# A planned attention and feed-forward kernel: a DMA ring model in its planner, shared tail casts, more XN buffers, and AV one unit late

## The chip, the cores and the metric

The kernel runs on one core of a Trainium2 chip. The metric is the device time of one execution in microseconds (us). An execution counts as slow when it is over 1.5% above the fastest of the same kernel (or when a die runs at a lower clock); only fast ones are compared.

The engines are TensorE (PE; its weight loads are shown apart as PEld), VectorE (DVE), ScalarE (ACT), GpSimd (POOL) and SyncE (SP). SP issues every DMA of this kernel, in one fixed order.

## The reference

Attention in a window of 32 positions to each side, for 8 batches of 576 tokens with 8 heads of 64, then a feed-forward layer of 512 to 2048 to 512 on all 4608 tokens.

```python
scores = (q @ k.transpose(0, 1, 3, 2)) / sqrt(64)        # q, k, v: (8, 8, 576, 64) float32
scores = where(abs(i - j) <= 32, scores, -1e9)
x = softmax(scores) @ v                                  # then (4608, 512)
r = maximum(x @ w_in, 0)                                 # w_in: (512, 2048)
out = (s * r * r + b) @ w_out                            # w_out: (2048, 512)
```

## The kernel before

No engine's program is written down by hand. Each operation is added to a graph with a cost, the data that it reads and writes, and a key (its priority). A planner in the kernel, ordinary Python that runs while the kernel is built, orders the graph: at each step it takes the task that can start first by its estimates. The result is one fixed list for each engine. On the chip every engine runs its list in order and waits on semaphores, so a wrong estimate can't give a wrong result, but a task that stands too early makes everything behind it wait.

```python
def plan(self, rounds=5):
    self.land = {}
    for _ in range(rounds):
        self._order()          # make the lists, with the landing times of the last round
        self._rings()          # serve the DMAs first in, first out: new landing times

# in _rings, for each DMA served:
    self.land[j[0].n] = now + 1100.0 - j[0].start      # kept relative to the DMA's start

# in _order, for each task taken:
    free[t.stream] = st + t.cost
    if t.dma is not None:
        t.fin = st + self.land.get(t.n, t.cost + 1800.0 + t.dma[1] * t.dma[2])
    ...
    elif t.dma is not None:
        r = t.fin + 100.0 + u.slack                    # when a user of the data may start
```

Here `t.dma[1]` is the number of units of a transfer and `t.dma[2]` the ns of one unit.

Batches 0 and 1 are transposed on PE. For batches 2 to 7, Q and K come in pieces of 512 and 64 rows: a load into STG, a cast to bf16 into NAT, a DMA transpose, and for K a reordering copy on POOL. V has its own loads and casts. A unit is a tile of 128 positions: its scores go through the exponential (ACT) and the mask (DVE), then AV multiplies them with V, DVE normalizes into one of the XN buffers, and a transpose (on PE for batches 0 to 2, by DMA after that) puts the result into XT for the feed-forward layer.

```python
NSTG, NNAT, NEX, NXN, NR1, NOUT, XR = 8, 6, 5, 3, 3, 6, 2048
LAG = 2                                   # AV of unit u rides with the scores of unit u+2
for name in names:                        # chunk(): "q" and "k", for 512 rows and for 64 rows
    add("sp", ... load STG ..., 500.0, dma=("l", np_ // 2, 53.0))
    add("dve", ... cast STG to NAT, 2048 wide ..., 110 + 0.53 * 2048, slack=3000.0)
    add("sp", ... transpose NAT ..., dma=("t", np_, 22.0))
    ... POOL copies of K, slack=2000.0
```

The softmax here doesn't subtract the row's maximum and nothing guards it: scores larger than these inputs give would overflow.

## Time and profile before

| | before |
|---|---|
| median of 3 runs, later of 4 | 333.91 us, 333.4 us |
| span of the profiled execution | 332.1 us |
| PE busy, idle | 305.5 us, 26.6 us |

The view by stretches of the kernel before, in four stretches; the columns are the stretch and its length in us, busy us (and instructions) of PE, PEld, DVE, ACT and POOL, the granted PE clock, the DMA share and GB/s.

```profile
0.00:60.00 60.00, 46.77 (x992) 37.30 (x992) 40.05 (x84) 31.78 (x53) 27.20 (x42) 1.00 1.02 303
60.00:105.00 45.00, 42.88 (x515) 24.29 (x516) 34.06 (x62) 19.55 (x30) 10.39 (x10) 1.00 1.07 207
105.00:165.00 60.00, 52.71 (x628) 24.61 (x627) 42.19 (x86) 29.61 (x44) 10.45 (x10) 0.94 0.92 194
165.00:180.00 15.00, 15.00 (x153) 7.14 (x151) 11.06 (x21) 6.59 (x10) 0.00 (x0) 1.00 1.29 216
```

The length less the PE column is PE's idle time: 13.23, 2.12, 7.29 and 0 us. After 180 us PE is idle for 4.0 us more, nearly all of it the tail.

### The profile page before, as it was taken

How to read it: one execution, taken by the hardware profiler on the slowest of the kernel's cores; microseconds unless marked ns; L12 is line 12 of the kernel's file. 1: busy time of each engine (PE TensorE's matmuls, PEld its weight loads, DVE VectorE, ACT ScalarE, POOL GpSimd, SP SyncE). 2: the span in 40 equal slices, each digit the busy share in tenths (PEclk: the TensorE clock that was granted, in tenths of full speed). 3: DMA queues.
4: the chain of work that ended last, by engine and by line, in shares of the span. 5: the costliest groups of instructions: out<-in, count | busy, mean ns of one | idle time of the engine just before them, and what ended most of it. 6: DMA issues, size and time to landing. Idle time of an engine off the chain costs nothing.

```text
span 332.1 us, 8135 instructions
## 1 busy us (share of the span) xinstructions
PE 305.5 (92%) x3452; PEld 162.2 (49%) x3452; DVE 204.7 (62%) x396; ACT 141.1 (42%) x219; POOL 59.0 (18%) x72
## 2 busy tenths in 40 slices
PE   3687999899989996988999999999999999999995
PEld 3565787654445443433445444444544444444442
DVE  2865768857887884858667865995654443333321
ACT  4644574246435653543444444444544323333300
POOL 3446444005050004100500600040000000000000
PEclk9999999999999999899799999999999999999999
DMA  7999999899999966998899879973121111100021
GB/s 255 288 307 353 335 273 343 145 200 238 197 179 310 222 139 116 287 149 172 245 211 172 208 210 201 169 192 113 45 59 49 49 43 44 53 33 34 34 84 74
DMA packets 104581, 56.71 MB, mean 171 GB/s; under 512 B 77216, under 2 KB 96160, under 8 KB 104544
## 3 DMA queue, kind: packets, MB, share of 16 engines
q1 hardware_dynamic: 104544, 56.18, 72.8%
q8 instruction: 27, 0.44, 0.6%
q14 instruction: 10, 0.08, 0.1%
HBM read 36.70 MB, written 9.44 MB: 139 GB/s over the span
## 4 chain that ended last, share of the span: by engine, by line
PE 58%; DMA 28%; DVE 6%; issue 3%; SPq 2%; POOL 1%; ACT 1%; DVEq 0%
PE o L815 28%; PE w L797 24%; DMA stg<-in_k_dram 7%; DMA vst<-in_v_dram 6%; DMA stg<-in_moe_w_out_dram 5%; DMA xt<-xn 3%; PE avn L597 3%; DMA stg<-in_moe_w_in_dram 2%; DMA qt<-nat 2%; DVE gt L806 2%; DVE nat L504 2%; DMA ktr<-nat 1%; PE o L838 1%; PE sc L541 1%; DVE xn L619 1%
## 5 line engine op out<-in xcount | busy, mean ns | idle before, releaser
L815 PE MATMUL o<-wout,gt 128*128 128x512 bf16 (+1 forms) x640 | 146.2, 361 | 2.8 <-DVE gt L806 1.8
L797 PE MATMUL w<-xt,win 128*128 128x512 bf16 (+3 forms) x704 | 147.9, 346 | 0.9 <-ACT xt L631 0.9
L804 ACT ACTIVATE r<-w 128x512 bf16<-128x512 f32 (+2 forms) x152 | 87.2, 574 | 111.0 <-PE w L797 90.9
L806 DVE TENSOR_TENSOR gt<-r 128x512 bf16<-128x512 bf16 (+2 forms) x152 | 68.9, 459 | 69.8 <-ACT r L804 69.3
L815 PEld LDWEIGHTS o<-wout,gt 128*128 128x128 bf16 x640 | 61.6, 98 | 65.9 <-DVE gt L806 2.3
L797 PEld LDWEIGHTS w<-xt,win 128*128 128x128 bf16 x704 | 60.8, 100 | 58.5 <-issue 2.4
L518 POOL COPY kt<-ktr 128x512 bf16<-128x512 bf16 (+1 forms) x30 | 31.8, 1059 | 135.2 <-DMA ktr<-nat 134.1
L567 ACT ACTIVATE ex<-sc 128x1024 bf16<-128x1024 f32 (+1 forms) x35 | 35.7, 1021 | 35.3 <-PE avn L597 33.9
L828 DVE SCALAR_TENSOR_TENSOR outs<-o,sb,cvec 128x512 f32<-128x512 f32 (+1 forms) x40 | 27.4, 690 | 13.0 <-PE o L815 13.0
L504 DVE CAST nat<-stg 128x2048 bf16<-128x2048 f32 (+1 forms) x24 | 29.7, 1246 | 7.2 <-DMA stg<-in_k_dram 6.0
L597 PE MATMUL avn<-vb,ex 64*64 64x65 bf16 x976 | 22.1, 199 | 8.4 <-DVE xn L619 4.5
L571 DVE TENSOR_TENSOR ex<-ex,mask 128x1024 bf16<-128x1024 bf16 (+1 forms) x35 | 25.8, 739 | 2.4 <-ACT ex L567 1.1
L619 DVE TENSOR_TENSOR xn<-avn,rec 128x512 bf16<-128x512 f32 (+1 forms) x34 | 23.3, 686 | 4.7 <-DMA xt<-xn 3.9
L597 PEld LDWEIGHTS avn<-vb,ex 64*64 64x64 bf16 x976 | 14.4, 108 | 23.5 <-issue 8.7
L445 DVE CAST vb<-vst 128x512 bf16<-128x512 f32 (+1 forms) x32 | 14.5, 456 | 8.3 <-DMA vst<-in_v_dram 8.3
L541 PE MATMUL sc<-qt,kt 64*64 64x128 bf16 x504 | 14.9, 217 | 0.0
L617 DVE RECIPROCAL rec<-avn 128x8 f32<-128x8 f32 (+1 forms) x34 | 6.8, 200 | 8.1 <-PE avn L597 8.1
L465 PE MATMUL w<-ident,nat 64*64 64x64 bf16 x144 | 5.4, 239 | 6.2 <-ACT nat L458 4.5
L541 PEld LDWEIGHTS sc<-qt,kt 64*64 64x64 bf16 x504 | 9.8, 107 | 1.3 <-issue 0.9
L426 POOL CAST win<-stg 128x1024 bf16<-128x1024 f32 x8 | 8.5, 1068 | 8.9 <-DMA stg<-in_moe_w_in_dram 8.8
L631 ACT COPY xt<-avn 128x512 bf16<-128x512 bf16 (+1 forms) x9 | 4.8, 537 | 11.6 <-PE avn L626 11.6
L465 PEld LDWEIGHTS w<-ident,nat 64*64 64x64 bf16 x144 | 4.6, 151 | 6.9 <-ACT nat L458 4.5
(62 smaller groups left out, 96.8 us busy)
## 6 DMA issues: line engine op xcount, KB each, us to landing
vst<-in_v_dram SPq DMA_DIRECT2D x32, 256.0 KB, 5.4
out_dram<-outs SPq DMA_DIRECT2D x32, 256.0 KB, 2.2
stg<-in_q_dram SPq DMA_DIRECT2D x6, 1024.0 KB, 6.6
stg<-in_k_dram SPq DMA_DIRECT2D x6, 1024.0 KB, 11.2
stg<-in_moe_w_in_dram SPq DMA_DIRECT2D x8, 512.0 KB, 7.6
stg<-in_moe_w_out_dram SPq DMA_DIRECT2D x8, 512.0 KB, 9.1
stg<-in_q_dram SPq DMA_DIRECT2D x8, 288.0 KB, 5.7
stg<-in_k_dram SPq DMA_DIRECT2D x8, 288.0 KB, 6.1
```

The lines of the kernel that those rows point to most:

```text
L504: add("dve", lambda e, stg=stg, nat=nat: e.tensor_copy(nat.rearrange("p (i h d) -> p h i d", h=H, i=4), stg.rearrange("p (h i d) -> p h i ...
L518: add("pool", lambda e, c=c, w=w: e.tensor_copy(KT[slot][:, :, c:c + w].rearrange("p a (s i) -> p a s i", i=4), KTR[slot][:, :, :, c // 4: ...
L541: fns = [lambda e, pr=pr, j=j, hp=hp: e.matmul(SC[64 * (j % 2):64 * (j % 2) + 64, hp, pr * 128:pr * 128 + 128], lhsT=KT[slot][64 * hp:64 * ...
L567: add("act", lambda e, dst=flat_dst, src=flat_src: e.activation(dst, src, AF.Exp, bias=0.0, scale=0.125), 190 + 0.833 * 512 * len(hs), rea ...
L571: add("dve", lambda e, flat=flat, mask=mask: e.tensor_tensor(flat, flat, mask, ALU.mult), 130 + 0.53 * 512 * len(hs), reads=[("E", ei, hp, ...
L597: return [lambda e: e.matmul(av[64 * x:64 * x + 64, h, 0:D + 1], lhsT=buf[64 * g:64 * g + 64, h % 2, h // 2, c:c + 64], rhs=VB[slot][64 * ...
L619: add("dve", lambda e: e.tensor_tensor(XN[xi][0:p1, :].rearrange("p (a c) -> p a c", a=H), av[0:p1, :, 0:D], REC[ri][0:p1, :].rearrange("p ...
L797: add("pe", [lambda e, g=g, kc=kc: e.matmul(wt[:, g, :], lhsT=WIN_BF[:, kc, (f0 + g) * 128:(f0 + g + 1) * 128], rhs=XT[:, kc, t0 % XR:t0 % ...
L804: add("act", lambda e: e.activation(rt, wt, AF.Relu, bias=0.0, scale=1.0), 190 + 0.833 * ng * nt, reads=[("W", wb)], writes=[("R1", rb)], ...
L806: add("dve", lambda e: e.tensor_tensor(GT[gs][:, f0:f0 + ng, g0:g0 + nt], rt, rt, ALU.mult), 130 + 0.53 * ng * nt, reads=[("R1", rb)], wri ...
L815: add("pe", [lambda e, fc=fc: e.matmul(O[:, ob, 0:cn], lhsT=GT[gs][:, fc, g0:g0 + 128], rhs=WOUT_BF[:, fc, c0:c0 + cn], start=(fc == 0), s ...
L828: add("dve", lambda e: e.scalar_tensor_tensor(OUTS[us][:, 0:cn], O[:, ob, 0:cn], SB128[:, 0:1], CVEC[:, c0:c0 + cn], ALU.mult, ALU.add), 2 ...
```

## The change

Its intent: fewer and shorter casts on DVE, lists that put DMA-dependent work later, and buffers where DVE had to wait. It has five parts.

1. The planner models a full DMA ring: a DMA blocks SP until all but 160 of the units asked for so far, its own included, have been served. SLACK lets users of transfers start later still; some of the planner's costs (transposes, K copies) and the casts' key change a little too.
2. The 64-row tails of Q and K are loaded into one buffer and share a cast. Every cast is cut into two halves of 1024; those of batch 2 go to POOL.
3. Five XN buffers for three, five output buffers for six.
4. AV one unit late and not two.
5. New pacing of the loads.

```diff
-LAG = 2
+LAG = 1
-PACE = ((-1,-1,-1,-1),(-2,-2,-2,-2),(-2,-2,-2,-2))
+PACE = ((-1, -1, -1),) * 3
+CASTS = 20.0
+CASTE = (("pool", "pool"), ("dve", "dve"))
+SLACK = (3000.0, 4000.0, 5000.0, 5000.0)
+    RING = 160.0
     def plan(self, rounds=5):
-        self.land = {}
+        self.land, self.block = {}, {}
 ...  in _rings: note what the queue has served at each time, then
+        for t, upto in asked:
+            while i < len(served) and served[i][1] < upto - self.RING:
+                i += 1
+            if i < len(served):
+                self.block[t.n] = max(0.0, served[i][0] - t.start)
 ...  in _order:
-            free[t.stream] = st + t.cost
+            free[t.stream] = st + max(t.cost, self.block.get(t.n, 0.0))
-        NSTG, NNAT, NEX, NXN, NR1, NOUT, XR = 8, 6, 5, 3, 3, 6, 2048
+        NSTG, NNAT, NEX, NXN, NR1, NOUT, XR = 8, 6, 5, 5, 3, 5, 2048
 ...  chunk() becomes piece(); the third piece holds both tails:
+            for i, parts in enumerate(((("q", 0, 512, 0),), (("k", 0, 512, 0),), (("q", 512, 64, 0), ("k", 512, 64, 32)))):
+                piece(b, parts, key + 0.01 * i, [paced(b, PACE[min(b, 4) - 2][i])])
```

More of the change, by code (lines that the diff above doesn't have):

```diff
@@ L107, in _rings @@
         jobs = {"hw": [], "sw": []}
+        self.block = {}
+        served, asked, total = [(0.0, 0.0)], [], 0.0
         for t in self.order:
@@ L110, in _rings @@
                 r = "sw" if t.stream == "pool" else "hw"
+                if r == "hw":
+                    total += t.dma[1]
+                    asked.append((t, total))
                 jobs[r].append([t, t.start + t.cost + (300.0 if r == "hw" else 700.0), float(t.dma[1])])
@@ L124, in _rings @@
             now += step
+            if "hw" in live:
+                served.append((now - step, served[-1][1]))
+                served.append((now, served[-1][1] + step / cost))
             for r, j in live.items():
@@ L129, in _rings @@
                     at[r] += 1
+        i = 0
+        for t, upto in asked:
[3 more added lines that the diff above has]
+                self.block[t.n] = max(0.0, served[i][0] - t.start)
     def _order(self):
@@ L481, in q_later, with piece @@
             return QTS[b % 2].rearrange("p (i a) s -> p i a s", i=4)
-        def chunk(b, t0, n, key, names="qk"):
-            slot, np_, s0 = b % 2, n // 4, t0 // 4
-            if b < 4 and t0 == 0 and "q" in names:
+        def piece(b, parts, key, waits):
+            slot = b % 2
+            ring["stg"] += ring["stg"] % 2
+            ring["nat"] += ring["nat"] % 2
+            si, _ = take("stg", NSTG), take("stg", NSTG)
+            ni, _ = take("nat", NNAT), take("nat", NNAT)
+            stg = STGS[:, si:si + 2, :].rearrange("p x c -> p (x c)")
+            nat = NATS[:, ni:ni + 2, :].rearrange("p x c -> p (x c)")
+            stgr, natr = [("STG", si), ("STG", si + 1)], [("NAT", ni), ("NAT", ni + 1)]
+            top = max(p0 + n // 4 for _, _, n, p0 in parts)
+            add("sp", [lambda e, name=name, t0=t0, n=n, p0=p0: e.dma_start(
+                stg[p0:p0 + n // 4, :].rearrange("p (h c) -> p h c", h=H),
+                src_of[name][b, :, t0:t0 + n, :].rearrange("h (p i) d -> p h (i d)", i=4))
+                for name, t0, n, p0 in parts],
+                500.0 * len(parts), writes=stgr, key=key - 20.0, waits=waits,
+                dma=("l", sum(n for _, _, n, _ in parts) // 8, 53.0))
+            for x in (0, 1):
+                eng = CASTE[min(b, 3) - 2][x]
+                add(eng, lambda e, x=x: e.tensor_copy(
+                    nat[0:top, 1024 * x:1024 * x + 1024].rearrange("p (i h d) -> p h i d", h=H, i=2),
+                    stg[0:top, :].rearrange("p (h i d) -> p h i d", h=H, i=4)[:, :, 2 * x:2 * x + 2, :]),
+                    110 + (0.53 if eng == "dve" else 1.05) * 1024, reads=stgr, writes=[("NAT", ni + x)], key=key + CASTS, slack=SLACK[0])
+            for name, t0, n, p0 in parts:
+                np_, s0, xs = n // 4, t0 // 4, pieces(t0, t0 + n, 64)
+                dst = q_later(b)[:, :, :, 16 + s0:16 + s0 + np_] if name == "q" else KTR[slot][:, :, :, s0:s0 + np_]
+                add("sp", lambda e, dst=dst, p0=p0, np_=np_: e.dma_start(
+                    dst.rearrange("p i a s -> p (i a) s"), nat[p0:p0 + np_, :], transpose=True),
+                    2000.0 if n > 64 else 1200.0, reads=natr,
+                    writes=[("QT", slot, x, pr) for x in xs for pr in range(NPAIR)] if name == "q" else [("KTR", slot, t0)],
+                    key=key + 0.1, dma=("t", np_, 20.0))
+                if name == "q":
+                    continue
+                land["kt", b, t0] = g.tasks[-1]
+                for c in range(t0, t0 + n, 128):
+                    w = min(128, t0 + n - c)
+                    add("pool", lambda e, c=c, w=w: e.tensor_copy(
+                        KT[slot][:, :, c:c + w].rearrange("p a (s i) -> p a s i", i=4),
+                        KTR[slot][:, :, :, c // 4:(c + w) // 4].rearrange("p i a s -> p a s i")),
+                        100 + 5.5 * w, reads=[("KTR", slot, t0)],
+                        writes=[("KT", slot, x, pr) for x in pieces(c, c + w, 64) for pr in range(NPAIR)],
+                        key=key + 3.0, slack=SLACK[1])
@@ L487, in chunk, with later @@
+        def later(b, key):
+            slot = b % 2
+            if b < 4:
                 for c0, x in ((0, 0), (160, WIN + S)):
@@ L490, in chunk @@
                         key=key - 20.0)
-            for name in names:
-                ring["stg"] += ring["stg"] % 2
-                ring["nat"] += ring["nat"] % 2
-                si, _ = take("stg", NSTG), take("stg", NSTG)
-                ni, _ = take("nat", NNAT), take("nat", NNAT)
-                stg = STGS[0:np_, si:si + 2, :].rearrange("p x c -> p (x c)")
-                nat = NATS[0:np_, ni:ni + 2, :].rearrange("p x c -> p (x c)")
-                stgr, natr = [("STG", si), ("STG", si + 1)], [("NAT", ni), ("NAT", ni + 1)]
-                add("sp", lambda e, stg=stg, name=name: e.dma_start(
-                    stg.rearrange("p (h c) -> p h c", h=H),
-                    src_of[name][b, :, t0:t0 + n, :].rearrange("h (p i) d -> p h (i d)", i=4)),
-                    500.0, writes=stgr, key=key - 20.0,
-                    waits=[paced(b, PACE[min(b, 4) - 2][2 * (t0 > 0) + "qk".index(name)])], dma=("l", np_ // 2, 53.0))
-                add("dve", lambda e, stg=stg, nat=nat: e.tensor_copy(
-                    nat.rearrange("p (i h d) -> p h i d", h=H, i=4), stg.rearrange("p (h i d) -> p h i d", h=H, i=4)),
-                    110 + 0.53 * 2048, reads=stgr, writes=natr, key=key, slack=3000.0)
-                dst = q_later(b)[:, :, :, 16 + s0:16 + s0 + np_] if name == "q" else KTR[slot][:, :, :, s0:s0 + np_]
-                xs = pieces(t0, t0 + n, 64)
-                add("sp", lambda e, nat=nat, dst=dst: e.dma_start(
-                    dst.rearrange("p i a s -> p (i a) s"), nat, transpose=True),
-                    2200.0 if n > 64 else 1200.0, reads=natr,
-                    writes=[("QT", slot, x, pr) for x in xs for pr in range(NPAIR)] if name == "q" else [("KTR", slot, t0)],
-                    key=key + 0.1, dma=("t", np_, 22.0))
-                if name == "k":
-                    land["kt", b, t0] = g.tasks[-1]
-                    for c in range(t0, t0 + n, 128):
-                        w = min(128, t0 + n - c)
-                        add("pool", lambda e, c=c, w=w: e.tensor_copy(
-                            KT[slot][:, :, c:c + w].rearrange("p a (s i) -> p a s i", i=4),
-                            KTR[slot][:, :, :, c // 4:(c + w) // 4].rearrange("p i a s -> p a s i")),
-                            100 + 4.8 * w, reads=[("KTR", slot, t0)],
-                            writes=[("KT", slot, x, pr) for x in pieces(c, c + w, 64) for pr in range(NPAIR)],
-                            key=key + 3.0, slack=2000.0)
@@ L650, in pe_part @@
                     reads=[r for p in parts for r in p[1]], writes=[r for p in parts for r in p[2]], key=key,
-                    slack=1500.0, waits=waits)
+                    slack=1500.0 if key < due(2, 0) - 1 else SLACK[2], waits=waits)
             t.mark = mark
@@ L760, in attention @@
             for b in range(2, B):
-                for t0, n in ((0, 512), (512, 64)):
-                    chunk(b, t0, n, due(b, 0) - 24.0)
+                later(b, due(b, 0) - 24.0)
                 for t in range(NUNIT):
                     load_v(b, t, due(b, t) - 35.0, waits=[paced(b, PACEV[min(b, 4) - 2][t])] + ([land["kt", 2, 0]] if b == 2 else []))
-                    cast_v(b, t, due(b, t) - 4.0, EV2[t], 3000.0)
+                    cast_v(b, t, due(b, t) - 4.0, EV2[t], SLACK[3])
                 for u in range(NUNIT):
```

## The prediction

> **What bounds the kernel now.** The page comes first, for the balance of the engines and for where in the span TensorE is not full.
>
> ```profile
> PE 305.5 (92%) x3452; PEld 162.2 (49%) x3452; DVE 204.7 (62%) x396; ACT 141.1 (42%) x219; POOL 59.0 (18%) x72
> PE   3687999899989996988999999999999999999995
> PEclk9999999999999999899799999999999999999999
> DMA  7999999899999966998899879973121111100021
> ```
>
> TensorE (PE) is busy for 305.5 of 332.1 us and no other engine passes 62%, so what is to be won is the 26.6 us in which PE does nothing, plus any time it runs at a lowered clock. A slice is 8.3 us. The first seven slices (57 us) fill while weights and batches 0 and 1 arrive with the DMA row at 7 to 9. From slice 22 on PE is full. Between lie dips at slices 16 and 18, and the only low clock digits of the span (8 and 7), at slices 17 and 20.
>
> Second, the view by stretches gives the dips their size (columns: stretch, its length, busy time and instruction count of PE, PEld, DVE, ACT, POOL, then PE clock, DMA share, GB/s).
>
> ```profile
> 75.00:90.00 15.00, 14.35 (x139) 7.02 (x138) 12.12 (x22) 8.64 (x14) 4.33 (x5) 1.00 1.23 214
> 90.00:105.00 15.00, 13.65 (x235) 7.12 (x234) 12.30 (x24) 5.16 (x7) 5.06 (x5) 1.00 1.02 231
> 105.00:120.00 15.00, 14.82 (x191) 7.29 (x190) 12.71 (x28) 10.26 (x16) 0.00 (x0) 1.00 0.95 219
> 120.00:135.00 15.00, 11.28 (x127) 5.08 (x126) 8.54 (x18) 4.96 (x7) 5.25 (x5) 0.90 0.74 149
> 135.00:150.00 15.00, 13.39 (x180) 6.31 (x178) 10.09 (x20) 8.69 (x13) 0.00 (x0) 0.99 1.13 209
> 150.00:165.00 15.00, 13.22 (x136) 5.92 (x135) 10.85 (x23) 5.71 (x9) 5.20 (x5) 0.89 0.84 198
> 165.00:180.00 15.00, 15.00 (x153) 7.14 (x151) 11.06 (x21) 6.59 (x10) 0.00 (x0) 1.00 1.29 216
> ```
>
> Fifteen minus the PE column, from 75 to 165 us, is 0.65 + 1.35 + 0.18 + 3.72 + 1.61 + 1.78 = 9.29 us idle; one 0.38 us gap at 209 us makes it 9.67. The clock adds to this. Narrower stretches show it at 0.68 over the 5.3 us from 130.7 us and 0.66 over the 5.0 us from 158.0 us: 0.32 x 5.3 + 0.34 x 5.0 = 3.4 us. Each slow stretch follows a stall. So the middle holds about **13.1 us** that nothing in the arithmetic asks for.
>
> Third, PE in order of time, with the releaser of each gap in brackets:
>
> ```profile
> 92.84 1.90 PE L815 MATMUL o<-wout,gt 128*128 128x512 bf16 x8 [1.35 <-DVE gt L806]
> 124.98 0.32 PE L597 MATMUL avn<-vb,ex 64*64 64x65 bf16 x16 [1.19 <-POOL kt L518]
> 130.70 0.25 PE L597 MATMUL avn<-vb,ex 64*64 64x65 bf16 x6 [2.30 <-DVE xn L619]
> 145.23 0.32 PE L597 MATMUL avn<-vb,ex 64*64 64x65 bf16 x16 [1.61 <-DVE xn L619]
> 158.37 0.32 PE L597 MATMUL avn<-vb,ex 64*64 64x65 bf16 x16 [1.78 <-POOL kt L518]
> ```
>
> The engines named are messengers. VectorE (DVE) and GpSimd (POOL) in order of time show what they had waited for:
>
> ```profile
> 91.23 1.22 DVE L504 CAST nat<-stg 16x2048 bf16<-16x2048 f32 x1 [0.56 <-DMA qt<-nat]
> 129.62 0.43 DVE L445 CAST vb<-vst 128x512 bf16<-128x512 f32 x1 [3.65 <-DMA vst<-in_v_dram]
> 144.49 0.69 DVE L619 TENSOR_TENSOR xn<-avn,rec 128x512 bf16<-128x512 f32 x1 [3.87 <-DMA xt<-xn]
> 157.28 4.76 POOL L518 COPY kt<-ktr 128x512 bf16<-128x512 bf16 x4 [23.14 <-DMA ktr<-nat]
> ```
>
> Each engine runs one planned list in order, and each stall is a DMA-dependent instruction placed too early in a list. At 125.97 us DVE reaches a cast of V whose load lands 3.65 us later; the normalization behind it, which frees the PSUM bank, waits with it, and PE stalls for 2.30 us. At 140.6 us a normalization has no free XN buffer: all three await transposes, one of which takes 10.04 us in the chain of waits. At 91 us a cast that fills 16 partitions waits for a NAT pair and then runs 1.22 us ahead of a squaring for PE. At 157 us POOL waits for a transpose of K, issued at 152.52 us behind others in the DMA-issuing engine's list.
>
> **What the Trainium skill says.** (1) "TensorE: Matmul & The Clock Gate", section "The HAM clock gate (the "warmup" mystery)": an idle PE falls to half clock and needs a few us of activity to recover. The trace agrees: a group of eight matmuls at 133.11 us takes 2.90 us where others take 1.73. A stall of some 2 us can thus cost nearly twice its length. (2) "VectorE: DVE Perf Modes", section "The perf-mode tier table (the rule you actually need)": an fp32 copy of 2048 elements takes 1227 ns; here the 16-partition casts average 1196 ns and the 128-partition ones 1312 ns from 75 us on, so partitions are nearly free and a cast of 16 costs what one of 128 does. (3) "SBUF — State Buffer" calls the port pair of DVE and GpSimd an exclusive lock, taken by two-port copies and casts; this trace has POOL's K copies at 1059 ns on average with single ones up to 1659, which fits but does not prove it. No page that I read gives a depth at which DMA issue blocks. The trace has transposes whose issue takes 1.13 to 8.3 us, which is the effect the new plan models.
>
> **The change, part by part.**
>
> *Casts.* Batches 2 to 7 have four Q/K casts each, 24 in all, 29.7 us of DVE. Now one 32-partition cast serves both 64-row tails, and every cast is cut into halves of 1024. From 512 elements (420 ns, V cast) and 2048 (1196 ns) the slope is (1196 - 420) / 1536 = 0.51 ns an element, so a half is an estimated 0.68 us. Five batches keep six halves on DVE: 30 x 0.68 = 20.4 us. Batch 2's six halves go to POOL at 1068 ns each (row of the weight casts, the same size): 6.4 us. DVE loses 9.3 us, to about 195; POOL rises to about 65. PE is the bound, so little of the 9.3 us counts as such. What counts: DVE is held 0.68 us at a time and not 1.22, and the 91 us stall goes, since batch 2's casts leave DVE and three staging pairs now serve three pieces.
>
> *Plan.* It now blocks the issuing engine when 160 units are outstanding, and assumes that transferred data comes later still: 3 us later for casts, 4 for K copies, 5 for attention on PE and V casts (before: 3.0, 2.0, 1.5, 3.0). No instruction is added. Later places in the lists aim straight at the stalls of 2.30 us (V cast) and 1.19 and 1.78 us (K copy).
>
> *Five XN buffers for three, five output buffers for six.* This aims at the 3.87 us DVE wait that gives PE's 1.61 us. Stores take 2.2 us to landing in the median and come about every 7 us, so five are enough.
>
> *AV one unit late.* Scores of unit u now ride with AV of u-1 rather than u-2. They fall one unit (4 to 6 us) later against the same deadline, so K of batch 2 gets that much grace. For later batches the new pacing releases the loads one AV unit later as well, which takes most of it back. The exponential and mask (1.02 + 0.70 us) must fit between two units, at least 3.5 us apart.
>
> *Unchanged:* matmuls, bytes, the number of transposes, and everything up to 57 us but its order.
>
> *Sum.* 13.1 us is the ceiling in the middle. I credit: 130.70 us stall with its clock 2.3 + 1.7, all but 0.7: 3.3; 158.37 us with its clock 1.8 + 1.7, two thirds: 2.3; 145.23 us: 1.3; 92.84 us: 1.2; 124.98 us: 0.8. Together 8.9 us. 333.9 - 8.9 = **325.0 us**, 2.7% less.
>
> **The rivals.**
> *A new wait takes the place of the old.* AV just behind its exponential can be late in ACT's and DVE's queues; from 105 to 120 us, DVE is busy 12.7 of 15. A stall of 0.5 us in ten units would return 5 us: 330. For it: the tight queue. Against: the plan knows these durations.
> *DMA is the bound of the middle.* Its share is near 1 from 75 to 210 us with unchanged bytes, so the data may just not come sooner. Then transfers move and PE stalls elsewhere: 330 to 333. Against: from 165 to 195 us the share is as high and PE is full, so work is at hand to cover late data if the order is right.
> *The plan gains elsewhere.* The ring model also reorders the first 57 us, where PE is idle for about 13 us; that could move the end by 2 us either way. With all the stalls gone besides, 319 to 321.
>
> **Range and chances.** Centre 325.0 us. Full recovery gives 320.8; a third gives 329.5. I take 320.5 to 330.0 for 8 in 10. Faster by over 2% means below 327.2, or 6.7 of the 13.1 us: 0.62. Within 2%: 0.35. Slower by over 2% needs a plan badly off: 0.03.
>
> **What would show it.** If right: PE idle from 75 to 165 us falls from 9.3 to under 4 us with no clock digit under 9 there; DVE busy about 195 and POOL about 65; no DVE wait on a transpose of XN; Q/K casts near 0.68 us on DVE; PE busy time falls by the clock loss only, to about 302. Wrong if PE shows new gaps released by the mask or exponential, if gaps on K copies stay or grow as loads start later, or if the first 57 us lengthen.

## The result

The changed kernel is **slower**: 343.69 us (median of 4, 341.81 to 346.76) against 333.4 us (median of 4, 331.4 to 334.08). The ratio is 1.033, with a 95% interval from 1.024 to 1.042. Ratios here are the mean time of one kernel's fast runs over that of the other's of the same rounds, so they are not quite the ratio of the medians. The prediction said 325.0 us with a range to 330.0.

The page of the changed kernel:

```profile
PE 305.3 (89%) x3452; PEld 163.2 (48%) x3452; DVE 195.8 (57%) x402; ACT 141.6 (41%) x219; POOL 67.0 (20%) x78
PE   3685599986879998999869999999999999999996
PEclk9999699999999999999979999999999999999999
DMA  7999599969996999499979968999411210110012
```

PE does the same work in the same busy time (305.3 us, 305.5 before), so the 9.0 us of span are idle time. DVE's busy time fell and POOL's rose as the prediction worked out. New are the hole at slices 4 and 5, at 26 to 43 us, in the second of which the DMA row has a 5 as well, and the weak slices up to 12. The view by stretches gives their size:

```profile
0.00:60.00 60.00, 41.46 (x820) 32.38 (x820) 35.99 (x72) 28.02 (x49) 27.52 (x40) 0.94 0.95 281
60.00:105.00 45.00, 37.12 (x573) 24.08 (x574) 30.09 (x66) 21.78 (x32) 12.48 (x13) 1.00 1.01 198
105.00:165.00 60.00, 58.05 (x671) 27.96 (x669) 40.70 (x85) 28.37 (x41) 10.76 (x10) 1.00 0.91 185
165.00:180.00 15.00, 10.91 (x119) 5.20 (x118) 6.35 (x16) 4.35 (x7) 5.32 (x5) 0.89 0.81 205
```

| PE idle, us | before | changed | difference |
|---|---|---|---|
| 0 to 60 us | 13.23 | 18.54 | +5.3 |
| 60 to 105 us | 2.12 | 7.88 | +5.8 |
| 105 to 165 us | 7.29 | 1.95 | -5.3 |
| 165 to 180 us | 0 | 4.09 | +4.1 |

From 105 to 165 us the change does what it was meant to do. It loses twice that in the first 105 us, though the prediction had said that up to 57 us nothing but the order changes. PE of the changed kernel in order of time, the three largest gaps after the start, with their releasers:

```profile
37.77 0.69 PE L484 MATMUL sc<-ident,nat 64*64 64x64 bf16 x18 [5.11 <-DVE nat L478]
98.48 0.40 PE L657 MATMUL avn<-ident,xn 128*128 128x128 bf16 x4 [2.44 <-DVE xn L650]
173.31 0.32 PE L628 MATMUL avn<-vb,ex 64*64 64x65 bf16 x6 [4.09 <-POOL kt L539]
```

The first gap is the transposition of the first K of batch 1. DVE, which casts that K, waits for its load (DVE of the changed kernel in order of time):

```profile
37.26 0.46 DVE L478 CAST nat<-stg 128x576 bf16<-128x576 f32 x1 [5.26 <-DMA stg<-in_k_dram]
```

The chain of work that ended last names the load, issued at 30.01 us and landed at 37.23 us:

```profile
30.01 7.22 DMA stg<-in_k_dram
```

In the kernel before, the load comes only 0.9 us earlier (issued at 29.09 us, landed at 36.33), but PE's list has the transposition later, behind feed-forward groups, and PE reaches it at 37.91 us without a gap:

```profile
37.91 0.75 PE L465 MATMUL sc<-ident,nat 64*64 64x64 bf16 x36
```

The stall also costs transfers. SP in order of time shows no issue between 32.02 and 39.81 us, since a staging buffer comes free only when its cast has been done. The wait is released by POOL's cast of a piece of the second weight at 38.75 us, and that cast stands in POOL's list behind a cast of Q that waits for its load (POOL of the changed kernel in order of time):

```profile
38.02 0.67 POOL L478 CAST nat<-stg 128x576 bf16<-128x576 f32 x1 [8.12 <-DMA stg<-in_q_dram]
```

In the kernel before, two such weight casts run first, at 31.91 and 34.91 us. The loads behind it start 5 to 6 us later (V of batch 1 at 42.47 us, before 36.41 us; Q of batch 2 at 51.36, before 46.63).

**What the planner believed.** Its own figures, printed while the kernel was built, can be set beside the trace. The changed planner has this K starting at 25.67 us and landing at 28.65; the trace has 37.23. For the kernel before it is 36.02, against 36.33 in the trace. So the new planner, which was to make transfers later, has them far too early. The repeats show why. In each round `block` is worked out from the starts of that round, while `land` is kept as the time after the start. In round 4 the blocks hold SP back: this load starts at 33.04 us and lands 2.98 us after its start. With starts so late the new blocks are near nothing. So in round 5 it starts at 25.67, keeps the 2.98, and lands at 28.65, although the planner's own queue has it landing only at 36.02. The rounds swing between the two pictures:

| round | 1 | 2 | 3 | 4 | 5 (used) |
|---|---|---|---|---|---|
| changed: planned end, us | 319 | 896 | 320 | 713 | 320 |
| changed: of 188 transfers, over 1 us too early by the planner's own queue | 136 | 6 | 117 | 9 | 96 |
| before: planned end, us | 325 | 381 | 321 | 330 | 322 |
| before: of 194 transfers, over 1 us too early | 145 | 19 | 91 | 31 | 29, none in the first 60 us |

After 30 rounds the changed planner has 1 of 188 too early, and a planned end of 325 us.

### The profile page after: what moved, and what is told of

The parts are those of the page before. It is cut to its first block, busy times and chain, and to the rows that moved or that the text cites. A ratio compares the mean times of both kernels' runs of the same rounds, so it can differ in the third digit from the quotient of the medians.

```text
span 341.1 us, 8141 instructions
## 1 busy us (share of the span) xinstructions
PE 305.3 (89%) x3452; PEld 163.2 (48%) x3452; DVE 195.8 (57%) x402; ACT 141.6 (41%) x219; POOL 67.0 (20%) x78
## 4 chain that ended last, share of the span: by engine, by line
PE 76%; DMA 13%; DVE 5%; SPq 2%; POOL 2%; issue 1%; ACT 1%; POOLq 0%
PE o L845 35%; PE w L827 32%; DMA vst<-in_v_dram 5%; DMA stg<-in_k_dram 4%; PE avn L628 4%; DMA stg<-in_moe_w_in_dram 3%; PE sc L572 2%; DMA ktr<-nat 1%; PE o L868 1%; DVE gt L836 1%; PE sc L484 1%; POOL nat L522 1%; DVE xn L650 1%; DVE ex L714 1%; SPq L472 1%
## 5 line engine op out<-in xcount | busy, mean ns | idle before, releaser
L827 PE MATMUL w<-xt,win 128*128 128x512 bf16 (+3 forms) x704 | 149.8, 345 | 3.9 <-issue 2.0
L836 DVE TENSOR_TENSOR gt<-r 128x512 bf16<-128x512 bf16 (+2 forms) x152 | 70.4, 469 | 82.1 <-ACT r L834 81.5
L522 DVE CAST nat<-stg 128x1024 bf16<-128x1024 f32 (+1 forms) x30 | 20.0, 680 | 4.7 <-DMA stg<-in_k_dram 2.4
L464 DVE CAST vb<-vst 128x512 bf16<-128x512 f32 (+1 forms) x32 | 13.6, 433 | 10.4 <-DMA vst<-in_v_dram 10.1
L478 DVE CAST nat<-stg 128x576 bf16<-128x576 f32 x8 | 4.1, 512 | 9.9 <-DMA stg<-in_k_dram 9.9
L484 PE MATMUL sc<-ident,nat 64*64 64x64 bf16 x144 | 3.8, 211 | 5.1 <-DVE nat L478 5.1
```

The lines of the kernel that those rows point to most:

```text
L522: add(eng, lambda e, x=x: e.tensor_copy(nat[0:top, 1024 * x:1024 * x + 1024].rearrange("p (i h d) -> p h i d", h=H, i=2), stg[0:top, :].re ...
L827: add("pe", [lambda e, g=g, kc=kc: e.matmul(wt[:, g, :], lhsT=WIN_BF[:, kc, (f0 + g) * 128:(f0 + g + 1) * 128], rhs=XT[:, kc, t0 % XR:t0 % ...
L836: add("dve", lambda e: e.tensor_tensor(GT[gs][:, f0:f0 + ng, g0:g0 + nt], rt, rt, ALU.mult), 130 + 0.53 * ng * nt, reads=[("R1", rb)], wri ...
```

## The experiments

**Theory U:** the slowdown comes from the planner's loop, which no longer settles in five rounds, so that the lists are made for transfers that land too early. **Rival P:** some part of the change costs by itself (POOL casts, AV one unit late, pacing). **Rival R:** the ring model is wrong for this chip even when settled. Each kernel below was timed against the kernel before, whose median was 333.3 to 335.1 us.

### One number: 30 rounds

```diff
-    def plan(self, rounds=5):
+    def plan(self, rounds=30):
```

> The changed kernel with one number changed: the planner repeats its estimate 30 times, not 5. Theory U (the ring model keeps the planner's loop from settling, so the lists are made for transfers that land too early; the plan used has 96 of 188 transfers over 1 us earlier than its own queue model serves them, with 30 repeats only 1): 322 to 332 us, the 5.1 us TensorE gap at 38 us gone, idle from 0 to 105 us back near 15 us. Rival P (a part of the change costs by itself: POOL casts, AV one unit late, pacing): stays at 340 to 346 us. Rival R (the ring model misdescribes the chip even when settled): also 338 us or more.

Measured: 333.71 us (331.86 to 336.15), ratio to the kernel before 0.9995 (0.991 to 1.008). The view by stretches:

```profile
0.00:60.00 60.00, 46.91 (x979) 38.16 (x980) 37.14 (x82) 30.91 (x52) 29.44 (x42) 1.00 1.00 299
60.00:105.00 45.00, 40.47 (x468) 22.47 (x465) 30.71 (x57) 18.66 (x28) 15.91 (x16) 0.99 0.98 197
```

PE's idle time up to 60 us is back at 13.1 us (13.2 before the change) and the gap at 38 us is gone. Nothing but the order of the lists differs from the changed kernel, so the loss of 3% is the order's. A part that costs 3% whatever the order (P) and a ring model that is wrong even when settled (R) fall as causes of it. U's lower figures were too hopeful: PE is still idle for 4.5 us from 60 to 105 us (2.1 before the change), and the settled version equals the kernel before and doesn't beat it.

### No ring limit

```diff
-    RING = 160.0
+    RING = 1e9
```

> The changed kernel with the ring limit set so high that it never blocks, 5 repeats as before; 7 of 188 transfers are then over 1 us too early. U: 325 to 333 us. P: 340 to 346 us. R: 325 to 333 us, and faster than the run with 30 repeats by 5 us or more.

Measured: 334.37 to 340.80 us in four executions, two of them slow; the ratio of the fast ones is 1.006 (0.994 to 1.019). The result is noisy, and U's 325 to 333 us are missed (the two fast runs have 334.37 and 337.88), but no run reaches even the changed kernel's fastest time (341.81). Without the limit five rounds suffice for a nearly settled plan, and most of the loss goes as well, from 3.3% to between -0.6 and 1.9%. R, by which this would beat the 30 rounds, has nothing for it.

### The new planner alone, on the kernel before

```diff
 (the kernel before)
+    RING = 160.0
+    (plan, _rings and _order of the changed kernel, 5 rounds)
```

> The kernel before with nothing but the new planner (ring model, 5 repeats); 94 of 194 transfers are then over 1 us too early in the plan. U and R: 338 to 350 us, with a TensorE gap of several us at about 38 us. P: 331 to 336 us as before.

Measured: 354.11 us (353.14 to 354.51), ratio 1.060 (1.051 to 1.069). The planner alone makes the old kernel 6% slower, more than the 338 to 350 us expected. PE in order of time has the same gap at 38 us, and a far larger one:

```profile
38.63 0.69 PE L481 MATMUL sc<-ident,nat 64*64 64x64 bf16 x18 [4.30 <-DVE nat L475]
70.97 0.61 PE L642 MATMUL avn<-ident,xn 128*128 128x128 bf16 x4 [10.77 <-DVE xn L635]
```

So the loss does not need the other parts of the change; with them beside the new planner it is smaller (3.3% and not 6.0%).

### AV two units late again, planner as changed

```diff
-LAG = 1
+LAG = 2
```

> The changed kernel with AV two units late again, ring model and 5 repeats kept; 111 of 188 transfers too early. U and R: no recovery, 337 to 350 us. P with the lag as its cause: 333 us or less.

Measured: 356.09 us (353.91 to 357.50), ratio 1.066 (1.057 to 1.074). There is no recovery, and the time lies above the expected 337 to 350 us; the lag isn't the cause. In this unsettled plan the longer lag goes with a larger loss; whether by itself or by the order that came of it isn't shown.

### The new planner on the kernel before, settled

```diff
 (as the new planner alone, but)
-    def plan(self, rounds=5):
+    def plan(self, rounds=30):
```

> The kernel before with the ring model and 30 repeats; none of 194 transfers too early, against 94 at 5 repeats. U: the loss of the run with the ring model and 5 repeats goes, 327 to 336 us. R (the ring model itself is wrong for this chip): stays at 345 us or more.

Measured: 332.53 us (332.18 to 334.05), ratio 0.996 (0.990 to 1.003). From 354 to 333 us by the number of rounds: U holds on both kernels, and R is refuted. A settled ring model is worth no more than the measurement's noise here.

### The kernel before with 30 rounds

> The kernel before with 30 planner repeats (no ring model); with 5 repeats 29 of its 194 transfers are over 1 us too early in the plan, all after 60 us; with 30 none. U: same or a little faster, 328 to 334 us. Rival V (any reordering costs several us, settled or not): 338 us or more.

Measured: 335.83 us (335.08 to 339.0), ratio 1.007 (0.999 to 1.015). Settling the old plan changes nothing that can be measured; its 29 early transfers all lie after 60 us. Rival V of the expectation (338 us or more) isn't borne out.

### Parts of the change under a settled plan

AV two units late again, with 30 rounds:

> The changed kernel with 30 repeats and AV two units late again. If AV one unit late is worth what the prediction gave it: 2 us or more slower than the changed kernel with 30 repeats (that was 333.7 us). If it costs, because each normalization, transpose and copy of batch 2 now stands right behind its exponential: 3 us or more faster, and the stalls from 100 to 107 us gone.

Measured: 336.06 us (333.79 to 336.45), ratio 1.005 (0.998 to 1.012), against 0.9995 for the changed kernel with 30 rounds. The cost of the shorter lag that was looked for is not there. The gain stays open: the ratios differ by 0.5%, some 1.7 us, near the 2 us looked for but inside the intervals.

Batch 2's casts on DVE, with 30 rounds (`CASTE = (("dve", "dve"), ("dve", "dve"))`):

> The changed kernel with 30 repeats and batch 2's casts on VectorE, as for the other batches. If the POOL casts (about 1.04 us each and in line with the K copies) are what holds the settled version at 333.7 us: 3 us or more faster. If they are hidden: within 2 us of 333.7 us.

Measured: 330.23 to 338.33 us, ratio of the fast runs 0.993 (0.982 to 1.004). Only two of the four runs are fast, so this is inconclusive: no difference of 2% from the kernel before, either way.

Six output buffers, with 30 rounds (they fit beside five XN buffers):

> The changed kernel with 30 planner repeats and six output buffers again (it fits beside the five XN buffers). If the fifth-buffer limit costs (the profiles of the settled changed kernels show VectorE waiting 2.2 to 7.0 us on stores): 1.5 to 5 us faster than 333.7 us and no VectorE wait on stores. If it is hidden: 332 to 335 us.

Measured: 331.89 us (330.11 to 335.49), ratio 0.996 (0.991 to 1.002). DVE's waits for stores, 2.2 us with five buffers, are gone from the profile; the time differs by less than the noise.

### Where the predicted gain went

With the slowdown settled, a question stays: 8.9 us were predicted, and the settled kernel gives none. Its trace shows where a stall sits now. DVE of the changed kernel with 30 rounds, in order of time:

```profile
99.77 1.30 DVE L464 CAST vb<-vst 128x512 bf16<-128x512 f32 x1 [2.19 <-DMA vst<-in_v_dram]
```

This is the same fault as at 129.62 us in the kernel before, a V cast ahead of a normalization, in another place. The settled planner has this load landing at 93.59 us and, with the slack of 5 us, the cast at 98.69; the trace has 99.77. The table compares planned and measured landings (median, us late) by when they landed:

| landed at | before | changed | changed, 30 rounds | one-pass, calibrated (below) |
|---|---|---|---|---|
| 30 to 60 us | -0.2 | 8.0 | 0.9 | 0.1 |
| 60 to 90 us | 1.1 | 15.4 | 1.5 | -2.1 |
| 90 to 120 us | 3.8 | 18.8 | 5.0 | -1.0 |

Even a settled plan drifts to 5 us late by 90 to 120 us, as much as the slack. One cost stands out: a 1 MB load of Q or K counts 64 x 53 = 3.4 us in the planner, and in seven traces such a load lands 4.5 us (median of 84) after the DMA in front of it. The next kernel therefore computes the queue in one pass while the lists are made, so that there is nothing to settle, and counts 70 ns a unit. It has six output buffers.

```diff
-        for _ in range(rounds):
-            self._order()
-            self._rings()
+        self._order()            # _issue() serves each DMA as SP issues it: start, block and landing agree
-                dma=("l", sum(n for _, _, n, _ in parts) // 8, 53.0))
+                dma=("l", sum(n for _, _, n, _ in parts) // 8, 70.0))
-        ... NOUT ... = 8, 6, 5, 5, 3, 5, 2048
+        ... NOUT ... = 8, 6, 5, 5, 3, 6, 2048
```

> The changed kernel, six output buffers, the queue model computed in one pass while the lists are made (so no repeats that could fail to settle), and the cost of a 1 MB load of Q or K set to 70 ns a unit as measured (about 4.5 us) in place of 53 (3.4 us). If transfers that land 5 to 10 us after the settled plan's time are what takes the gain from 90 us on: 322 to 330 us, stalls between 75 and 165 us under 5 us in all. If the transfers bound the middle anyway: 331 to 336 us.

Measured: 330.69 us (328.61 to 331.74), ratio 0.993 (0.988 to 0.999). This lies between the two ranges of the expectation, and the stalls from 75 to 165 us are 9.8 us, not under 5. The estimates now fit, and the stalls do not go: they gather. One stretch of the view by stretches, first of this kernel:

```profile
90.00:120.00 30.00, 21.59 (x330) 11.75 (x332) 18.96 (x35) 12.26 (x17) 5.49 (x5) 0.77 0.73 181
```

then of the kernel before:

```profile
90.00:120.00 30.00, 28.48 (x424) 14.40 (x423) 25.01 (x50) 15.41 (x22) 5.06 (x5) 1.00 0.99 225
```

PE is idle for 8.4 us of these 30, where the kernel before has 1.5, and from 120 to 165 us for 1.3 where that has 7.1. The planner expects it: its own lists hold 9.1 us of PE idle time between 90 and 120 us. The reading, tested below, is that PE has run out of work that doesn't need batch 2.

The same planner on the parts of the kernel before:

> The kernel before with that same one-pass, calibrated planner and none of the other parts. Compared with a_cal it gives what casts, XN buffers, slacks, pacing and lag are worth together under a plan that knows the transfers. The prediction's view of the parts: 4 us or more slower than a_cal. The view that only the order counts: within 3 us of a_cal.

Measured: 329.04 us (328.16 to 330.90), ratio 0.990 (0.985 to 0.995). It is within noise of the version with all parts (0.993). So under a plan that knows the transfers, casts, buffers, slacks, pacing and lag together are worth nothing that can be measured. This version is about 1% faster than the kernel before (0.5 to 1.5%).

AV two units late, on the one-pass version:

> As a_cal with AV two units late again. AV one unit late gains as predicted: 2 us or more slower than a_cal. It costs: 2 us or more faster. Else within 2 us.

Measured: 331.84 us (330.24 to 333.12), ratio 0.997 (0.991 to 1.002). It is 0.3% above the one-pass version, some 1.1 us, which is within noise.

Five XN buffers, on the one-pass version of the kernel before:

> The one-pass, calibrated planner on the kernel before (b_cal, 329.0 us) with five XN buffers for three. The profile of b_cal has VectorE waiting 2.4 us on transposes of XN and 2.3 us at most at once for V loads. If the XN wait still reaches TensorE: 1 us or more faster than b_cal and no such wait. If it is hidden under the right order: within 1.5 us of it.

Measured: 330.20 us (329.19 to 334.87), ratio 0.985 (0.982 to 0.989), against 0.990 (0.985 to 0.995) without. The two were timed in different jobs and the intervals overlap, so a gain of 0.5% (1.6 us, the size looked for) is neither shown nor excluded.

### Does the arrival of data bound the middle?

**Theory D:** it does. Two kernels move fewer bytes and change no instruction on any engine but the length of DMAs. The planner is told of the shorter transfers, though, and makes new lists: of PE's 391 places, 135 hold another task than in the one-pass version in the first kernel, and 36 in the second. Their outputs are wrong, which doesn't matter for the times. The first fetches half of each row of Q and K for batches 2 to 7:

```diff
-    stg[...] <- src[...]                    # rows of 256 floats
+    stg[...][:, :, 0:128] <- src[...][:, :, 0:128]
-                dma=("l", ... // 8, 70.0))
+                dma=("l", ... // 8, 38.0))
```

> Wrong result on purpose: as a_cal, but the Q and K loads of batches 2 to 7 fetch only half of each row (the rest of the staging buffer is stale), and the plan knows it. Same instructions on every engine. If the arrival of batch 2's data bounds the stretch from 90 to 120 us (theory D): that stretch loses 5 us or more of its idle and slow-clock time, 321 to 326 us against 330.7 for a_cal. If it is the chain of instructions alone or the order: 328 to 332 us.

Measured: 322.84 us (321.66 to 324.39), ratio to the kernel before 0.964 (0.960 to 0.967). Against the one-pass version's 0.993 this is 0.964 / 0.993 = 0.970, some 10 us less. (The output still passes the comparison, most likely since the scores are small, so that wrong ones barely move the averages. The result is wrong by construction all the same.) The same stretch of the view by stretches:

```profile
90.00:120.00 30.00, 27.95 (x423) 14.00 (x422) 21.43 (x46) 16.21 (x23) 4.36 (x5) 0.94 0.74 181
```

The idle time of 8.4 us is down to 2.05 and the clock is up from 0.77 to 0.94.

The second fetches an eighth of the bytes of four of the sixteen weight loads, all of them before batch 2's transfers:

> Wrong result on purpose: as a_cal, but four of the sixteen weight loads fetch an eighth of their bytes, so that about 5 us of transfers go before 60 us and all of batch 2's transfers can come earlier. D: 321 to 327 us, the stalls from 90 to 120 us shrink although nothing of batch 2 was touched. Else: 328 to 332 us.

Measured: 324.99 us (321.99 to 327.02), ratio 0.967 (0.963 to 0.971); the output is wrong. Nothing of batch 2 was touched, and the time falls by 0.967 / 0.993, about 9 us. Both times are what theory D expected: the middle waits for the bytes of batch 2, which stand in one queue behind the weights and batches 0 and 1. But 9 us is more than the about 5 us of transfers taken out (an estimate from the planner's costs), and the lists differ too. How much is the earlier arrival alone, and how much the order made for it, was not separated; that would take the same lists with fewer bytes.

## Why the prediction was wrong

**The bound and the stalls.** Right: PE is the bound, and idle time decides. From 105 to 165 us the idle time fell from 7.3 to 1.95 us. PE's busy time was to fall to about 302 us with the slow stretches gone; it stayed at 305.3, as new gaps brought new slow stretches (mean clock 0.984, before 0.990).

**The casts.** Right in size: 0.680 us for a half (0.68 estimated), DVE 195.8 us (about 195), POOL 67.0 us (about 65). As said, little of it counts.

**The plan: the step that failed.** "Later places in the lists aim straight at the stalls" took the intent of the new model for its effect. The repeat loop was in the listing, five rounds of it, and the prediction did not ask whether it still settles with `block` taken from one round's starts and `land` from another's. It doesn't: the plan used had 96 of 188 transfers over 1 us too early, the first K of batch 1 at 28.65 and not 37.23 us, and the work that needs such loads stands too early, not later, in the lists of PE, DVE and POOL. The number of rounds alone takes the loss away (343.7 to 333.7 us). The rival that named the place, "the plan gains elsewhere", gave the first 57 us "2 us either way"; the first 60 us lost 5.3 us of PE time, and 11 are lost up to 105 us. "Slower by over 2% needs a plan badly off" was right as a condition, and 0.03 was too little for it. Two of the signs of being wrong came: the first 57 us lengthened, and a gap on K copies grew (4.09 us at 173 us; 1.19 and 1.78 before). New gaps released by the mask or the exponential did not.

**XN and output buffers.** Half right. The DVE wait on XN transposes (3.9 us) is in no trace of a kernel with five buffers, and is 2.4 to 4.9 us in four of the five with three (the new planner alone has none). "Five are enough" for the stores was too hopeful: with 30 rounds DVE waits 2.2 us on them, 7.0 with the longer lag as well. Six do not always help: the new planner on the kernel before, settled, has 2.4 us with six. In time, neither is visible.

**AV one unit late.** Under settled plans two units late measure 0.5% and 0.3% slower, within noise both times: a gain of 1 to 2 us is neither shown nor excluded.

**The sum.** 8.9 us were credited to single stalls, as if each gap were lost for its own reason. With the plan settled the gain is 0.0 us (ratio 0.9995, by its interval within 3 us either way), with a calibrated plan 0.7%. The rival "DMA is the bound of the middle" had it: "then transfers move and PE stalls elsewhere: 330 to 333". The argument against it, that PE is full from 165 to 195 us at as high a DMA share, was taken from a later stretch. It is also half misread: the share is 1.29 from 165 to 180 us but 0.76 from 180 to 195, where PE is full too. Between 90 and 120 us the calibrated plan finds no work to fill PE with, and taking bytes out, with the lists made anew for it, is what moved the idle time there (8.4 to 2.05 us).

What stays open: why the five-round plan costs 6% on the old parts and 3.3% on the new ones. Both plans are unsettled, and their errors were not followed one by one. Open too is how much of the gain of the two kernels with fewer bytes is arrival and how much order.

## What to carry to other kernels

A planner that iterates on its own estimates must be shown to settle: print the planned end of each round, and compare planned with measured landings in the trace before crediting it with anything. A stall that names an engine, then a buffer, then a transfer is worth what the transfer's arrival allows: here the best orders moved the stalls and took away 1 to 1.5%, while fewer bytes took 3% more. Cutting bytes on purpose, with the same instructions, is a cheap test of that, and a sharper one with the lists held fixed.

## What the Trainium skill lacked or had wrong

- DMA issue: no page that was read gives the depth at which a full ring blocks the issuing sequencer. In the changed kernel with 30 rounds a single DMA transpose holds SP for 6.08 us and five V loads together for 8.11 us.
- "DMA: Bandwidth & Descriptors", section "Bandwidth": its row for 1 MB gives 6.15 us and 341 GB/s, which do not go together (1 MB in 6.15 us is about 170 GB/s); in all four rows of the table the rate is twice the size over the time. Here a 1 MB load of Q or K, issued by SP in 1 KB pieces into a busy queue, lands 4.5 us after the DMA in front of it in the median, about 230 GB/s.
- "TensorE: Matmul & The Clock Gate", section "The HAM clock gate (the "warmup" mystery)": it speaks of an idle window of about 3.4 us before the clock falls. In the kernel before, gaps of 2.30 and 1.78 us were followed by slow stretches (granted clock 0.68 over 5.3 us and 0.66 over 5.0 us), while one of 2.44 us in the changed kernel was not. So in this trace a single gap under 3.4 us was enough, and its length alone does not tell.
